# First loads on other queues, fewer and shorter dummy matmuls, and two transposes turned behind a product

## The chip, the cores and the metric

The kernel runs on one core of one Trainium2 chip. A core has a matrix engine (TensorE, in the profile PE for its matmuls and PEld for its weight loads), three engines for elementwise work (VectorE, DVE in the profile; ScalarE, ACT; GpSimd, POOL), and SyncE (SP), which here only issues transfers. ScalarE can issue transfers too. Each engine works through its own instructions in order and waits on semaphores for the others. The transfers of all queues are carried out by 16 DMA engines. The metric is the device time in microseconds (us); lower is better.

## What is computed

Attention with a polynomial sketch for 16 heads (4 batches of 4 heads, 1088 positions, 32 wide), and behind it a feed-forward layer with a squared ReLU:

```python
def phi(x):                                   # 64 features of each position
    a = einsum('rd,bhsd->bhsr', S1, x)        # S1, S2: 8 x 32
    b = einsum('rd,bhsd->bhsr', S2, x)
    return einsum('bhsi,bhsj->bhsij', a, b).reshape(..., 64)
q_p, k_p = phi(q), phi(k)
kv  = einsum('bhsf,bhsd->bhfd', k_p, v)
z   = sum(k_p, axis=2)
num = einsum('bhsf,bhfd->bhsd', q_p, kv)
den = einsum('bhsf,bhf->bhs', q_p, z)[..., None] + 1e-06
x   = (num / den).transpose(0, 2, 1, 3).reshape(4352, 128)
out = relu(x @ w_in) ** 2 @ w_out             # w_in 128 x 2048, w_out 2048 x 128
```

All arrays are float32.

## The kernel before, in words

The feed-forward part is by far the larger one: 4352 rows, cut into ten chunks (`FC`) of 256 to 512 columns of the transposed x, each going through 16 slices of 128 hidden units (lines 600 and 644). The attention of a batch has to be ready before the feed-forward of its rows. For most of the program an order of the instructions is planned by a small list scheduler (`_Order`), which is given durations and due times. The head of the program, which makes the first 256 columns of x from batch 0, is written out by hand, and the change lies in this head alone. Each engine runs the head's instructions in the order in which the source issues them.

What the head does, with the names that matter here:

- Loads. Before the change ScalarE's queue issues S1 and S2 into `s_nat` (L225, L226), 8 rows each. SyncE's queue issues, in this order: k of batch 0, columns 0 to 512 (the first range) and 512 to 1088 (the second range), each over 128 partitions (L181); the first part of q, 256 columns (L187); eight loads of v (L199), four for its first range of tiles (0 to 4) and four for its second (4 to 9); then more of q, the two weight matrices in quarters (L208, L217), the rest of q, and the loads of the next batches. Every transfer has one of eight semaphores, given out in turn in the order of the program. A transfer that gets a semaphore for the second time is issued only after the first transfer with it has landed; for SyncE the fourth load of v is the first of these.
- Dummies. TensorE has nothing to do until S has landed. `keep_warm(n, cols)` issues n matmuls of 128 x `cols` on constants, whose result nobody reads (L695). Seven of 512 columns stand ahead of the first real matmuls, and one of 384 behind them.
- S. Eight matmul instructions (L706) bring S1 and S2 into `sp`, in the forms in which they are used, and ScalarE copies that to `ss` (L709). Everything below needs `ss`.
- k. VectorE transposes k into `kt0` (L293, `a_kT0`): tiles 0 and 1, 2 and 3 (both of the first range), 4 to 6, 7 and 8 (of the second range). TensorE forms the sketch of k from it, in four groups `kf` of the same tiles (L318, `a_kf`), ScalarE copies one half of each (`kb`, L324), and VectorE multiplies the halves into `kp` (L334, `a_kp0`).
- q. VectorE transposes the first 256 columns of q (L299, `a_qT`), and TensorE forms both sketches of q with the 64 features spread out (L757, `q0`).
- kv and z. 72 matmul instructions sum kp times v over the nine tiles into `kvp` (L399, `a_kv0`), eight for each tile; those of tiles 0 to 3 need v's first range, the rest its second.
- Behind it follow, each short and each waiting for the one before: masks of kvp, den (L826), num (L831), the reciprocal, and the first 256 columns of `xT` (L854). Then the first feed-forward matmuls start (L600).

In the order of the source, VectorE transposes all of k, then q, and then forms the products `kp`. The lines that the listing does not explain by itself:

```python
W0, W1, W3 = 7, 0, 1                 # dummies: ahead of S, behind S, ahead of the first L600
new_kp(0)
a_kf(0, 2, psf, "po")                # TensorE, then ScalarE
a_qT(0, 0, 8)                        # VectorE
a_kp0(0, 2)                          # VectorE
```

Of the kernel before, what the change touches and what calls it, by code (L numbers as in the profile page):

```python
# [14 lines left out]
def _ap(t: bass.AP, p0: int, np_: int, off: int, free):  # L15
    p = list(t.ap)[0]
    return bass.AP(
        t.tensor, t.offset + p0 * p[0] + off, [[p[0], np_]] + [list(d) for d in free]
    )
# [88 lines left out]
def kernel(  # L108
# [11 lines left out]
    nc = tc.nc  # L120
# [7 lines left out]
    GT, G2, LA = 4, 6, 3.5  # L128
    LU = 4
    KC = [(0, 160), (160, 128)]  # L130
    W0, W1, W3 = 7, 0, 1
    ND, QT, WI, KL, QL = 2, 6.0, (1.0, 1.9), (30.0, 8.0), 4.0


# [25 lines left out]
    def sb(name, cols, dt=F32, rows=128):  # L160
        return cpool.tile([rows, cols], dt, tag=name, name=name)
# [10 lines left out]
    s_nat, ss, s2f = sb("s_nat", 32, rows=16), sb("ss", 80), sb("s2f", 32)  # L172
# [7 lines left out]
    def load_k(eng, b, c0=0, c1=S):  # L180
        eng.dma_start(  # L181
            kn[b % 2][:, c0:c1],
            bass.AP(k.tensor, k.offset + b * H * S * D + c0, [[G * D, 128], [1, c1 - c0]]),
        )

    def load_q(eng, b, c0, c1):
        eng.dma_start(  # L187
            qn[b % 2][:, c0:c1],
            bass.AP(q.tensor, q.offset + b * H * S * D + c0, [[G * D, 128], [1, c1 - c0]]),
        )  # L190
# [3 lines left out]
    def first(b, t, p):  # L194
        return NT * p + t if b else 4 * p + t if t < 4 else 16 + 5 * p + t - 4
# [26 lines left out]
            ),  # L222
        )

    nc.scalar.dma_start(s_nat[0:8, :], S1[:, :])  # L225
    nc.scalar.dma_start(s_nat[8:16, :], S2[:, :])  # L226
    load_k(nc.sync, 0, 0, 512)
    load_k(nc.sync, 0, 512, S)
    load_q(nc.sync, 0, 0, 256)
    for t0, t1 in ((0, 4), (4, NT)):  # L230
        for p in range(4):
            load_v(nc.sync, 0, p, t0, t1)
# [57 lines left out]
    def a_kT0(t0, n):  # L290
        p = 3 if t0 + n > NT - 2 else 4
        i = 32 * (first(0, t0, 1) - first(0, t0, 0))
        nc.vector.transpose(  # L293
            _ap(kt0, 0, 128, 128 * t0, [[32, p], [128, n], [1, 32]]),
            _ap(kn[0], 0, 128, 32 * first(0, t0, 0), [[i, p], [32, n], [1, 32]]),
        )

    def a_qT(b, i0, n):
        nc.vector.transpose(qT[:, 32 * i0 : 32 * i0 + 32 * n], qn[b % 2][:, 32 * i0 : 32 * i0 + 32 * n])  # L299
# [13 lines left out]
    def a_kf(t0, n, pool, tag, w=32):  # L313
        kf = pool.tile([128, 512], F32, tag=tag, name="kf")
        for t in range(n):
            for c in range(0, 128, w):
                o = 128 * (t0 + t) + c
                nc.tensor.matmul(  # L318
                    _ap(kf, c, w, 32 * t, [[32 * n, 2], [1, 32]]),
                    kt0[:, o : o + w],  # L320
                    sf,
                )
        kb = wpool.tile([128, 32 * 3], F32, tag="kb", bufs=4, name="kb")
        nc.scalar.copy(kb[:, 0 : 32 * n], kf[:, 32 * n : 64 * n])  # L324
        st["kf", t0] = kf, kb

    def new_kp(b):

        st[b, "kp"] = wpool.tile([128, 64 * NT * H], F32, tag="kp", name="kp")

    def a_kp0(t0, n):

        kf, kb = st["kf", t0]
        nc.vector.tensor_tensor(  # L334
            out=_ap(st[0, "kp"], 0, 128, 256 * t0, [[64, 4 * n], [8, 8], [1, 8]]),
            in0=_ap(kf, 0, 128, 0, [[8, 4 * n], [1, 8], [0, 8]]),
            in1=_ap(kb, 0, 128, 0, [[8, 4 * n], [0, 8], [1, 8]]),
            op=mult,
        )
# [352 lines left out]
    def keep_warm(n, cols=512):  # L692
        t_ = st["warm"]
        for _ in range(n):
            nc.tensor.matmul(  # L695
                t_[:, 0:cols],
                nc.const_aps.tensor(1.0, (128, 128), mybir.dt.bfloat16),
                nc.const_aps.tensor(1.0, (128, cols), mybir.dt.bfloat16),
            )
# [17 lines left out]
    for c in range(2, 4):  # L717
        load_wo(nc.sync, c)
    load_q(nc.sync, 0, 640, S)
    keep_warm(W1)  # L720
    keep_warm(1, 384)
    a_kT0(0, 2)
    a_kT0(2, 2)
    for x in range(2):
# [21 lines left out]
    nc.gpsimd.memset(_ap(pd, 0, 128, 8, [[9, 4 * NT], [1, 1]]), 1e-6)  # L746

    a_kT0(4, 3)
    a_kT0(7, 2)


    x0 = att("x0")
# [9 lines left out]
    qp0 = wpool.tile([128, 512], F32, tag="qp0", bufs=1, name="qp0")  # L762
    new_kp(0)
    a_kf(0, 2, psf, "po")
    a_qT(0, 0, 8)
    a_kp0(0, 2)
    a_kf(2, 2, psf, "pg")
    a_kf(4, 3, psf, "po")
    a_kf(7, 2, psf, "pg", 64)
# [402 lines left out]
```

## Time and profile before

| what | value |
|---|---|
| median of 3 runs | 183.94 us (183.80 to 184.47) |
| the profiled execution's own time | 184.05 us |
| its span, first to last instruction | 182.2 us |
| TensorE busy | 177.6 us, 97% of the span |
| VectorE, ScalarE, GpSimd busy | 121.8, 136.5, 38.6 us |
| first real matmul (L706) | at 4.08 us |
| sketch of k (L318), sketch of q (L757), kv (L399) start | at 4.94, 6.71, 7.33 us |
| first feed-forward matmul (L600) | at 12.32 us |

Times inside the profile count from the start of the span. The profiled execution's own time is 1.85 us longer than its span. A busy TensorE is not TensorE at its full speed, since its clock can be held at half; the profile gives the clock that was granted only as far as it was recorded. A wait of an instruction for several semaphores is put down to the one that came last by the profile, which need not be the real one.

### The profile page before, as it was taken

What the parts mean: (1) busy time and instruction counts of PE and PEld (TensorE: products, weight loads), DVE (VectorE), ACT (ScalarE), POOL (GpSimd) and SP (SyncE); (2) the same over time, 40 slices, a digit from 0 to 9 for tenths busy, and PEclk for the clock granted to TensorE, in tenths of its full rate; (3) what the DMA queues carried; (4) which work ended last, traced back from release to release, by engine and by line L of the source; (5) the groups of instructions that cost most, each with busy time, mean ns of one, the idle gap of its engine ahead of it and who ended that gap; (6) DMA issues with size and microseconds to landing.
All of it is one profiled execution on the core that took longest, in us unless ns stands there. A gap on an engine that the chain in (4) does not pass through costs nothing.

```text
span 182.2 us, 3996 instructions
## 1 busy us (share of the span) xinstructions
PE 177.6 (97%) x1529; PEld 104.7 (57%) x1529; DVE 121.8 (67%) x262; ACT 136.5 (75%) x259; POOL 38.6 (21%) x158
## 2 busy tenths in 40 slices
PE   7999999999999999999999999999999999999992
PEld 2868776656555655655555554545454555555792
DVE  4989779999999961899994335996353334333640
ACT  3439579759947886799937778995777777777980
POOL 3546118348200003470018000600000000000000
PEclk9999999999999999999999999999999999999999
DMA  5799995010028900000031200003003000300211
GB/s 167 199 275 324 213 261 136 8 31 0 0 43 217 204 0 4 4 2 0 0 54 23 35 0 5 0 0 59 0 4 58 0 0 6 51 0 0 35 26 29
DMA packets 26146, 11.26 MB, mean 62 GB/s; under 512 B 17936, under 2 KB 25104, under 8 KB 26128
## 3 DMA queue, kind: packets, MB, share of 16 engines
q1 hardware_dynamic: 25936, 10.95, 25.5%
q8 instruction: 12, 0.20, 0.5%
q10 hardware_dynamic: 192, 0.07, 0.1%
q14 instruction: 6, 0.05, 0.1%
HBM read 8.78 MB, written 2.23 MB: 60 GB/s over the span
## 4 chain that ended last, share of the span: by engine, by line
PE 96%; DMA 2%; DVE 0%; issue 0%; ACT 0%; ACTq 0%
PE po L644 61%; PE pg L600 18%; PE nd L553 3%; PE po L639 2%; PE pol L639 2%; PE qc L306 2%; DMA kn<-in_k_dram 2%; PE nd L417 1%; PE kvp L399 1%; PE kf L318 1%; PE qc L350 1%; PE kvp L417 1%; PE nd L350 0%; PE x L757 0%; PE den L826 0%; PE x L443 0%
## 5 line engine op out<-in xcount | busy, mean ns | idle before, releaser
L644 PE MATMUL po<-g,w_o 128*128 128x512 f32 (+3 forms) x288 | 122.7, 546 | 0.0
L612 ACT ACTIVATE gt<-pg 128x512 f32<-128x512 f32 (+3 forms) x144 | 75.2, 570 | 31.4 <-PE pg L600 30.9
L644 PEld LDWEIGHTS po<-g,w_o 128*128 128x128 f32 x288 | 53.4, 189 | 31.8 <-issue 24.8
L600 PE MATMUL pg<-xT,w_in 128*128 128x512 f32 (+3 forms) x160 | 70.0, 518 | 0.0
L623 ACT ACTIVATE g<-gt 128x512 f32<-128x512 f32 (+2 forms) x102 | 60.7, 623 | 1.6
L625 DVE TENSOR_TENSOR g<-gt 128x512 f32<-128x512 f32 (+3 forms) x43 | 30.0, 699 | 39.5 <-ACT gt L612 38.8
L600 PEld LDWEIGHTS pg<-xT,w_in 128*128 128x128 f32 x160 | 29.1, 190 | 28.8 <-ACT gt L612 11.6
L513 POOL COPY rd<-rc 32x9 f32<-32x9 f32 (+2 forms) x80 | 19.1, 239 | 26.8 <-DVE rc L505 23.5
L459 POOL COPY kv<-kvt 32x64 f32<-32x64 f32 x48 | 12.7, 264 | 44.7 <-DVE kvt L436 42.5
L522 DVE STREAM_SHUFFLE qa<-qc 128x576 f32<-128x576 f32 (+2 forms) x20 | 11.8, 648 | 0.0
L537 DVE TENSOR_TENSOR qp<-qa,qb 128x576 f32<-128x576 f32 (+2 forms) x20 | 10.8, 603 | 0.0
L485 DVE STREAM_TRANSPOSE qt<-qc 128x576 f32<-128x576 f32 (+2 forms) x10 | 5.8, 610 | 5.6 <-PE qc L350 3.8
L370 DVE TENSOR_TENSOR kp<-fs 128x576 f32<-128x576 f32 x12 | 8.7, 738 | 0.0
L648 DVE STREAM_TRANSPOSE oT<-po 128x512 f32<-128x512 f32 (+3 forms) x9 | 5.9, 653 | 2.1 <-PE po L644 2.1
L553 PE MATMUL nd<-qp,kv 32*32 32x288 f32 (+2 forms) x320 | 6.6, 354 | 0.0
L299 DVE STREAM_TRANSPOSE qT<-qn 128x192 f32<-128x192 f32 (+3 forms) x11 | 5.8, 555 | 0.6 <-DMA qn<-in_q_dram 0.6
L522 DVE STREAM_SHUFFLE qb<-qc 128x576 f32<-128x576 f32 (+2 forms) x10 | 6.1, 648 | 0.0
L570 DVE TENSOR_TENSOR xT<-nd,bc 128x576 fp32r<-128x576 f32 (+2 forms) x10 | 5.6, 592 | 0.5 <-PE nd L553 0.5
L639 PE MATMUL po<-w_o,g 128*128 128x128 f32 x32 | 5.8, 280 | 0.0
L639 PE MATMUL pol<-w_o,g 128*128 128x128 f32 x32 | 5.7, 275 | 0.0
L563 DVE STREAM_TRANSPOSE bc<-rd 128x576 f32<-128x576 f32 (+2 forms) x10 | 5.7, 596 | 0.0
L553 PEld LDWEIGHTS nd<-qp,kv 32*32 32x32 f32 x320 | 2.9, 103 | 3.6 <-issue 2.4
(106 smaller groups left out, 89.7 us busy)
## 6 DMA issues: line engine op xcount, KB each, us to landing
kn<-in_k_dram SPq DMA_DIRECT2D x3, 544.0 KB, 8.4
qn<-in_q_dram SPq DMA_DIRECT2D x3, 544.0 KB, 11.5
vn<-in_v_dram SPq DMA_DIRECT2D x9, 144.0 KB, 7.2
w_in<-in_moe_w_in_dram SPq DMA_DIRECT2D x4, 256.0 KB, 4.4
w_o<-in_moe_w_out_dram SPq DMA_DIRECT2D x4, 256.0 KB, 4.9
out_dram<-oT SPq DMA_DIRECT2D x12, 64.0 KB, 1.9
out_dram<-oT SPq DMA_DIRECT2D x8, 56.0 KB, 2.7
out_dram<-oT SPq DMA_DIRECT2D x8, 48.0 KB, 1.8
```

Source lines behind the costliest of these rows:

```text
L370: nc.vector.tensor_tensor(out=_ap(st[b, "kp"], 0, 128, 64 * NT * h, [[64, NT], [8, 8], [1, 8]]), in0=_ap(fs, 0, 128, o, [[32, NT], [1, 8], ...
L459: nc.gpsimd.tensor_copy(_ap(st[b, "kv"], 32 * c, 32, 64 * h, [[32, E], [1, 32]]), _ap(st["kvt"], 32 * h, 32, 0, [[64, E], [1, 32]]),)
L513: nc.gpsimd.tensor_copy(st[b, "rd", i0][32 * h : 32 * h + 32, n * c : n * c + n], st["rc"][32 * c : 32 * c + 32, n * h : n * h + n],)
L522: nc.vector.stream_shuffle(in_=banks(st[b, "qc", i0], 2 * x, 0, m), out=_ap(st[b, which, i0], 0, 128, 2 * m * x, [[m, 2], [1, m]]), mask=m ...
L537: nc.vector.tensor_tensor(out=st[b, "qp", i0, e][:, r], in0=st[b, f"qa{e}", i0][:, r], in1=st[b, "qb", i0][:, r], op=mult,)
L553: nc.tensor.matmul(nd[32 * h : 32 * h + 32, 512 * c : 512 * c + m], kv[r, o : o + 32], qp[r, m * h : m * h + m], start=(e == 0), stop=(e = ...
L600: nc.tensor.matmul(st["pg", u][:, n * i : n * i + n], w_in[:, 128 * (d0 + i) : 128 * (d0 + i) + 128], xT[:, c0 : c0 + n],)
L612: nc.scalar.activation(gt[:, 0:w], st["pg", u][:, 0:w], Relu)
L623: nc.scalar.activation(to, of, Square)
L625: nc.vector.tensor_tensor(out=to, in0=of, in1=of, op=mult)
L639: nc.tensor.matmul(po[x // 128][:, 0:128], g[:, x : x + 128], w, start=(d == 0), stop=(d == NB - 1),)
L644: nc.tensor.matmul(po[0][:, 0:n], w, g, start=(d == 0), stop=(d == NB - 1))
```

## The change

- k's first range and q's first part are issued by ScalarE's queue, in this order. S1 and S2 are issued by SyncE's queue, ahead of k's second range.
- Six dummies of 512 columns instead of seven stand ahead of the matmuls of S, and two of 160 columns instead of one of 384 behind them.
- On VectorE the transpose of k's last two tiles and the transpose of q stand behind the first product `kp`, no longer ahead of it.

The order of the semaphores follows the order of the program: k's first range now has the first, and the fourth load of v, which reuses it, waits for k's first range instead of S1. No other instruction is added, removed or moved on any engine; the planned part has the same order as before.

```diff
-    W0, W1, W3 = 7, 0, 1
+    W0, W1, W3 = 6, 1, 1
...
-    nc.scalar.dma_start(s_nat[0:8, :], S1[:, :])
-    nc.scalar.dma_start(s_nat[8:16, :], S2[:, :])
-    load_k(nc.sync, 0, 0, 512)
+    load_k(nc.scalar, 0, 0, 512)
+    nc.sync.dma_start(s_nat[0:8, :], S1[:, :])
+    nc.sync.dma_start(s_nat[8:16, :], S2[:, :])
     load_k(nc.sync, 0, 512, S)
-    load_q(nc.sync, 0, 0, 256)
+    load_q(nc.scalar, 0, 0, 256)
...
-    keep_warm(W1)
-    keep_warm(1, 384)
+    keep_warm(W1 + 1, 160)
     a_kT0(0, 2)
     a_kT0(2, 2)
...
     a_kT0(4, 3)
-    a_kT0(7, 2)
...
     new_kp(0)
     a_kf(0, 2, psf, "po")
+    a_kp0(0, 2)
+    a_kT0(7, 2)
     a_qT(0, 0, 8)
-    a_kp0(0, 2)
     a_kf(2, 2, psf, "pg")
```

## The prediction, made before the changed kernel was run

> **What bounds the kernel now.** The page comes first: how much of the span is TensorE (PE), and which chain ended last.
>
> ```profile
> PE 177.6 (97%) x1529; PEld 104.7 (57%) x1529; DVE 121.8 (67%) x262; ACT 136.5 (75%) x259; POOL 38.6 (21%) x158
> PE 96%; DMA 2%; DVE 0%; issue 0%; ACT 0%; ACTq 0%
> ```
>
> PE is busy for 177.6 of 182.2 us. None of the edits touches what runs after 13 us, so they can only move the moment from which PE has feed-forward work without a break (the first L600 at 12.32), and the end moves with it one for one. Next, the chain of waits in order of time, asked for the first 25 us (start, duration, what):
>
> ```profile
> 0.73 2.82 DMA kn<-in_k_dram
> ...
> 4.08 0.49 PE sp L706 x8
> 4.57 0.43 PE warm L695
> 5.01 1.77 PE kf L318 x64
> 6.78 0.62 PE x L757 x16
> 7.40 2.25 PE kvp L399 x72
> ```
>
> From 4.08 on the chain is PE without a gap up to the end of kvp (9.65); from there a string of short steps leads to 12.3, and the change doesn't touch it. So the question is when kvp ends. The timeline of the head says what each engine does (start, duration, engine, what; in brackets the idle time before and who ended it):
>
> ```profile
> 0.73 0.89 SPq L181 DMA_DIRECT2D kn<-in_k_dram  x2
> 0.73 0.60 ACTq L225 DMA_DIRECT2D s_nat<-in_S_dram  x1
> 0.77 3.15 PE L695 MATMUL warm<-const-bfloat16-1.0 128*128 128x512 bf16 x7 [0.77 <-PEq L1156]
> 1.37 0.29 ACTq L226 DMA_DIRECT2D s_nat<-in_S_dram  x1
> 3.58 0.77 DVE L293 STREAM_TRANSPOSE kt<-kn 128x256 f32<-128x256 f32 x2 [1.00 <-DMA kn<-in_k_dram]
> 4.08 0.49 PE L706 MATMUL sp<-sel,s_nat 16*32 16x80 f32 x8 [0.17 <-DVE kt L293]
> 4.54 0.84 DVE L293 STREAM_TRANSPOSE kt<-kn 128x384 f32<-128x384 f32 x2 [0.19 <-DMA kn<-in_k_dram]
> 4.63 0.23 ACT L709 COPY ss<-sp 128x80 f32<-128x80 f32 x1 [1.45 <-PE sp L706]
> 5.30 0.40 DVE L299 STREAM_TRANSPOSE qT<-qn 128x256 f32<-128x256 f32 x1
> 5.90 2.75 DVE L334 TENSOR_TENSOR kp<-kf,kb 128x512 f32<-128x512 f32 x4 [0.20 <-ACT kb L324]
> 6.71 0.69 PE L757 MATMUL x<-qT,sq 32*64 32x256 f32 x16
> ```
>
> Last, single lines and their waits; the rows of PEldq are TensorE's queue holding for semaphores, and the last two belong to the eighth load of v:
>
> ```profile
> L706 PEldq EVENT_SEMAPHORE  x2: 51/51/51, 2.2 to 4.0; - x2
> ...
> L318 PE MATMUL kf<-ss,kt x64: 219/314/316, 4.9 to 6.6; 128*32 128x64 f32 x56, 128*64 128x64 f32 x8
> ...
> L399 PEldq EVENT_SEMAPHORE  x4: 51/51/51, 6.7 to 8.1; - x4
> ...
> L199 SPq DMA_DIRECT2D vn<-in_v_dram x1: 430/430/430, 5.5 to 5.5; - x1
> ...
> DMA to landing us min/median/max: 2.6/2.6/2.6
> ```
>
> Three readings. (1) sp waited for S2: its queue holds until 2.2 (S1) and until 4.0 (S2), so the 0.17 that the timeline puts down to DVE is S2's landing. The dummies cover this: they start 0.43 apart, and the seventh ends at 3.7. (2) The matmuls of kf fall from 314 to 219 ns within the group; in the trace their bundles stand 0.107 apart up to 5.98 and 0.056 after it. PE runs at half speed until 5.98 (the page's clock row reads full throughout and doesn't show it). (3) kvp's second half (40 of 72 matmuls) waits for v's second range. Its last load was issued at 5.46 and landed 2.6 later, at 8.1; that half started at 7.33 + 32 x 0.029 = 8.25. From a release to the first load sp needed 0.08 (3.97 to 4.05), so the half could have started at 8.20: only 0.05 of slack.
>
> **The change, part by part.** I carry the sum on the profiled execution: 184.05 us, of them 182.2 span and 1.85 around it. It stands 0.11 above the median of the three runs (183.94).
>
> S1 and S2 first on SyncE, six dummies. S1, first on its queue, was seen by PE 1.5 after its issue; S2, issued 0.64 later behind the traffic of k, 2.6 after. An issue of 128 rows takes SP 0.43; S2's eight rows took ACT 0.29. On SP, S2 is issued at about 0.73 + 0.40 = 1.1, before most of k's traffic. Bounds for its arrival: 2.6 (S1's latency) and 3.7 (its own latency again). I take 3.2, the middle, since k's first range is issued at the same moment as before. Six dummies end at 0.77 + 6 x 0.43 = 3.35, so sp starts there and not at 4.08: -0.73. Two dummies of 160 columns (0.27 at half speed) replace one of 384 (0.32), between sp and the copy to ss, where PE waits anyway: nothing; without that wait they would cost 0.27. ss follows at 3.90 and kf could start at 4.20 (before 4.93).
> The Trainium skill, "DMA: Bandwidth & Descriptors", section "Issuing engines are not separate DMA queues", speaks against this step: transfers from all issuing engines share the same 16 DMA engines, so another queue saves issuing time only. By that rule alone S2 gains its 0.3 of earlier issue, kf would start at about 4.6, and the sum carried through DVE would be 184.3 instead of 184.2; the trace neither proves nor refutes it, since S1 (alone) and S2 (in traffic) differ by 1.1 in latency. The outcome with S2 late is rival A.
>
> k's first range first on ScalarE. SP's first issue took 0.41, ACT's first 0.60 (L225). So k lands between 3.55 (as now) and 3.74; I take 3.74, because L225 is the same place in the same queue. kt's first transpose ends 0.45 later and kf starts at 4.25: -0.68. ACT's table load (1.28) and the 0.20 copy slide from 1.69 to about 1.85 and end at 3.35, ahead of ss at 3.90: nothing; an issue 0.5 longer would use up that cover. q's first part landed at 5.04 and is now read at about 6.1: nothing.
>
> k's second range third on SP. Issue about 1.5 instead of 1.2, behind k's first range in the DMA engines as before. Landing between 4.51 (unmoved) and 5.04 (q, which took the 0.53 behind it, goes first). I take 4.70, k's own shift, because the first range holds the engines until then either way.
>
> kf, the order on DVE. kf's first two groups run at half speed from 4.25 to 5.1; kb is ready 0.94 after kf's start (5.87 before), at 5.19. DVE from k's landing: transpose of three tiles 0.50 (5.20), first kp 0.61 (5.81), last transpose 0.26 (6.07), qT 0.40 (6.47), three kp 2.14: 8.61, before 8.65. The swap fills the 0.20 that DVE idled ahead of the first kp, and that is all it gives. Behind the moved kp wait kf's last group (needs the transpose of 6.07) and L757 (needs qT): L757 at 6.57 and not 6.71, kvp at 7.19 and not 7.33: -0.14.
>
> v behind a new wait. On SP the fourth load of v reuses the semaphore of the first transfer in program order: S1 before, k's first range now. It was issued at 3.56; now it waits for k's landing, 3.74 to 3.76: +0.20. The other loads of v, the rest of q and all weights are queued behind it on SP; the weights have room (first cast 10.86, needed by 12.26). Bounds: 0 (k lands at 3.55) to +0.20. If the eighth load moves by 0.19 with it, it lands at 8.29 and kvp's second half starts at 8.39: +0.14 on 8.25. Its last kp (8.61) is in time for 9.09.
>
> Sum: PE and DVE would be 0.14 earlier, v makes it 0.14 later, and the later one decides: 184.05 + 0.14 = 184.19 in a profiled execution, 184.1 against the median. What the earlier S wins (0.73) is lost at two other landings: k's second range through DVE, and v's second range.
>
> **Rivals.**
> A, S2 lands no earlier. For: reading (1). Against: it is issued ahead of most of k. Then kf starts at 4.93 and the first kp at 5.90, but the last transpose and qT (0.66) now follow it: DVE ends 9.30, L757 starts at 7.2, kvp 0.5 late: 184.4.
> B, slower: TensorE stays at half speed. The clock rose at 5.98, after a stretch from 2.57 with 3.24 of 3.41 us counted busy (windows of the profile). The change removes 0.43 of dummies and opens gaps ahead of kf (0.25), at k's second range (0.2) and at the last transpose. If these are too many, PE stays slow for another such stretch, to 9.39: kf's rest +0.5, L757 +0.45, kvp twice as slow until then; kvp ends at about 10.95, not 9.65: 183.94 + 1.3 = 185.2. It decides where PE idles more than the window allows; before, 5 to 10% was allowed, now I count 14 to 20%. For the 3.41 stretch: the Trainium skill, "TensorE: Matmul & The Clock Gate" (Part 1), says the throttle is released after a busy, free-running window of about 3.4 us; the trace has one rise, at 5.98, which fits a window that began at 2.57.
> C, v is not late. SP spends 0.29 on each S instead of 0.43, k lands at 3.55, and the fourth load of v is not held. Then the -0.14 of PE stands, or -0.3 with a k that is early too: 183.7.
> D, clearly faster: the whole 0.73 arrives at the end and the half-speed stretch costs less behind it. This needs both ranges of k and v to land 0.7 earlier, while v's loads are issued 0.47 apart as before: 183.94 - 0.95 = 183.0.
>
> **How the numbers follow.** Chances: forecast 0.42, A 0.15, B 0.15, C 0.20, D 0.08. Half a per cent (0.92 us) is about what a measurement of this kernel can tell from no change. Forecast and C lie within it; so does A, except 0.02 in which its delay and some slow clock add up. Faster 0.08 (D), slower 0.17 (B and that share), same 0.75. The range takes the forecast, A, C and most of B: 183.3 to 185.2; D and the tail of B stay out. The likeliest case's own range is 183.8 to 184.4, from v's bounds (0 to +0.20) and the spread of the runs.
>
> **What would show it.** Right: TensorE's queue released for sp before 3.4; sp at 3.35 and kf near 4.25; the second k landing within 4.5 to 5.0 and no idle DVE ahead of the first kp; fourth load of v issued right after k's landing, L399's second half released at 8.2 to 8.4; kvp ending within 0.2 of 9.65. Wrong: S2 released near 4.0 (A); matmuls of L399 at half their speed (B); the eighth load of v well before 8.1 with kvp following it (C, D).

## The result, and the profile after

The changed kernel takes 186.06 us (median of 22 runs, 184.33 to 187.32); the kernel before, run beside it, 184.75 (22 runs, 183.80 to 185.83). The ratio is 1.0059, with a 95% interval of 1.0036 to 1.0083: slower, by an estimate just over the half per cent that the prediction set as its limit, with an interval that reaches to both sides of it; the median lies outside the prediction's range. The ratios in this document are of fast runs alone, without those more than 1.5% above the fastest of the same kernel (here one, of 187.32), which is why this one is below the ratio of the medians, 1.0071. The spread of the runs is part of the result: 3.0 us after, 2.0 before.

The profiled execution of the changed kernel happened to be one of its faster ones: 184.58 us, span 182.7, against 184.05 and 182.2 before. Its page comes first, with the engines and the chain that ended last:

```profile
PE 177.3 (97%) x1529; PEld 104.7 (57%) x1529; DVE 121.9 (67%) x262; ACT 136.6 (75%) x259; POOL 39.2 (21%) x158
PE 91%; DMA 5%; SPq 1%; POOL 0%; issue 0%; DVE 0%
```

PE's work is the same, but 5% of the chain is now transfers instead of 2%. The timeline of the head says which (start, duration, engine, what; idle time before it and who ended it):

```profile
0.73 0.41 SPq L226 DMA_DIRECT2D s_nat<-in_S_dram  x1
0.74 0.39 ACTq L181 DMA_DIRECT2D kn<-in_k_dram  x1
...
1.20 0.29 SPq L227 DMA_DIRECT2D s_nat<-in_S_dram  x1
...
1.53 0.36 SPq L181 DMA_DIRECT2D kn<-in_k_dram  x1
...
3.67 0.49 PE L706 MATMUL sp<-sel,s_nat 16*32 16x80 f32 x8 [0.18 <-DMA s_nat<-in_S_dram]
...
4.50 1.64 PE L318 MATMUL kf<-ss,kt 128*32 128x64 f32 x56
...
4.88 0.58 DVE L293 STREAM_TRANSPOSE kt<-kn 128x384 f32<-128x384 f32 x1 [0.64 <-DMA kn<-in_k_dram]
...
6.59 0.45 PE L318 MATMUL kf<-ss,kt 128*64 128x64 f32 x8 [0.45 <-DVE kt L293]
...
6.97 0.69 PE L755 MATMUL x<-qT,sq 32*64 32x256 f32 x16
...
7.59 2.32 PE L399 MATMUL kvp<-vn,kp 128*64 128x64 f32 x72
...
12.04 2.09 POOL L688 CAST w_in<-w_in 128x512 fp32r<-128x512 f32 x3 [4.52 <-DMA w_in<-in_moe_w_in_dram]
```

The matmuls of S start at 3.67 (before 4.08) and those of kf at 4.50 (4.94), so 0.4 is won at the front. Then VectorE idles 0.64 for k's second range, which lands at 4.84 (before 4.51); PE idles 0.45 ahead of kf's last group; and the sketch of q (line 755 here, 757 before) starts at 6.97, 0.26 later than before. From there kvp runs as before. In this execution the first quarter of w_in lands only at 11.98 (10.81 before), and the first feed-forward matmul waits about 0.45 more for its cast; it starts at 13.03 (12.32 before).

That the median lies 1.5 above this execution is not explained by it. So seven more executions of the changed kernel were profiled (after_again, after_p1 to after_p6). The trace records the granted clock of TensorE from the moment at which it first rises to full speed; that moment is the column "rise".

| execution | clock rise | k's 2nd range landed | kvp (L399), first and last start | first L600 | own time | own time - first L600 |
|---|---|---|---|---|---|---|
| before | 5.98 | 4.51 | 7.32, 9.42 | 12.32 | 184.05 | 171.73 |
| after_p3 | 4.14 | 4.76 | 7.41, 9.51 | 12.41 | 183.99 | 171.58 |
| after | 5.38 | 4.84 | 7.58, 9.68 | 13.03 | 184.58 | 171.55 |
| after_again | 9.48 | 4.84 | 8.38, 10.96 | 13.85 | 185.47 | 171.62 |
| after_p5 | 9.70 | 5.11 | 8.42, 11.08 | 13.98 | 185.63 | 171.65 |
| after_p2 | 9.84 | 5.68 | 9.00, 11.46 | 14.36 | 186.12 | 171.76 |
| after_p1 | 10.19 | 4.74 | 8.31, 11.24 | 14.14 | 186.03 | 171.89 |
| after_p4 | 11.82 | 5.37 | 8.69, 12.19 | 15.09 | 186.71 | 171.62 |
| after_p6 | 12.25 | 4.79 | 8.48, 12.27 | 15.17 | 186.80 | 171.63 |

(The times in the table are cut, not rounded, to hundredths, so they can be 0.01 below those in the lines of the profile.) The last column is constant within 0.35: what sets these executions apart happens ahead of the first L600. And of the eight executions of the same program the two whose clock rose by 5.4 lie at 184.0 and 184.6, the six whose clock rose after 9.4 at 185.5 to 186.8. The landing of k's second range doesn't sort them like that: it came earliest in after_p1 (4.74) and at 4.79 in after_p6, which took 186.03 and 186.80. One line of the kernel shows where the time goes. L399's matmuls in after_p3 (duration of one in ns, minimum, median and maximum; first and last start):

```profile
L399 PE MATMUL kvp<-vn,kp x72: 222/222/270, 7.4 to 9.5; 128*64 128x64 f32 x72
```

and in after_p4:

```profile
L399 PE MATMUL kvp<-vn,kp x72: 221/314/369, 8.7 to 12.2; 128*64 128x64 f32 x72
```

In after_p4 the 72 matmuls need 3.5 us from first to last start instead of 2.1, and they also start 1.28 later, 0.6 of it because k's second range landed later in this execution (5.37 against 4.76), as its timeline shows:

```profile
4.55 1.08 PE L318 MATMUL kf<-ss,kt 128*32 128x64 f32 x32
...
5.41 0.58 DVE L293 STREAM_TRANSPOSE kt<-kn 128x384 f32<-128x384 f32 x1 [1.08 <-DMA kn<-in_k_dram]
...
6.13 1.55 PE L318 MATMUL kf<-ss,kt 128*32 128x64 f32 x32 [0.49 <-DVE kt L293]
...
7.61 1.16 PE L755 MATMUL x<-qT,sq 32*64 32x256 f32 x16
...
8.70 3.72 PE L399 MATMUL kvp<-vn,kp 128*64 128x64 f32 x72
```

L755 takes 1.16 at half speed, 0.69 at full speed. The prediction's rival B is this case; it got a chance of 0.15 and a price of 1.3.

### The profile page after: what moved, and what is told of

It is laid out like the page before. It is cut to its first block, busy times and chain, and to the rows that moved or that the text cites. A ratio compares the mean times of both kernels' runs of the same rounds, so it can differ in the third digit from the quotient of the medians.

```text
span 182.7 us, 3996 instructions
## 1 busy us (share of the span) xinstructions
PE 177.3 (97%) x1529; PEld 104.7 (57%) x1529; DVE 121.9 (67%) x262; ACT 136.6 (75%) x259; POOL 39.2 (21%) x158
## 4 chain that ended last, share of the span: by engine, by line
PE 91%; DMA 5%; SPq 1%; POOL 0%; issue 0%; DVE 0%
PE po L644 61%; PE pg L600 18%; PE nd L553 3%; DMA w_in<-in_moe_w_in_dram 3%; PE po L639 2%; PE pol L639 2%; PE qc L306 2%; DMA kn<-in_k_dram 1%; PE nd L417 1%; SPq L199 1%; PE qc L350 1%; PE kvp L417 1%; PE nd L350 0%; POOL w_in L688 0%; PE warm L844 0%
## 5 line engine op out<-in xcount | busy, mean ns | idle before, releaser
L600 PE MATMUL pg<-xT,w_in 128*128 128x512 f32 (+3 forms) x160 | 70.1, 519 | 0.0
L600 PEld LDWEIGHTS pg<-xT,w_in 128*128 128x128 f32 x160 | 29.2, 190 | 28.4 <-ACT gt L612 11.5
L513 POOL COPY rd<-rc 32x9 f32<-32x9 f32 (+2 forms) x80 | 19.7, 246 | 25.8 <-DVE rc L505 22.6
L522 DVE STREAM_SHUFFLE qa<-qc 128x576 f32<-128x576 f32 (+2 forms) x20 | 11.8, 649 | 0.0
```

Source lines behind the costliest of these rows:

```text
L513: nc.gpsimd.tensor_copy(st[b, "rd", i0][32 * h : 32 * h + 32, n * c : n * c + n], st["rc"][32 * c : 32 * c + 32, n * h : n * h + n],)
L522: nc.vector.stream_shuffle(in_=banks(st[b, "qc", i0], 2 * x, 0, m), out=_ap(st[b, which, i0], 0, 128, 2 * m * x, [[m, 2], [1, m]]), mask=m ...
L600: nc.tensor.matmul(st["pg", u][:, n * i : n * i + n], w_in[:, 128 * (d0 + i) : 128 * (d0 + i) + 128], xT[:, c0 : c0 + n],)
```

## The experiments

Two theories stood at the start. *Clock:* the missing seventh dummy and the new gaps let TensorE's clock rise late in a part of the executions. *Landings:* the new queues make k's second range (or w_in) land later, whatever the clock does. Ratios are to the kernel before, run beside each kernel on the same chip, with 95% intervals; each kernel was run 9 to 12 times unless said otherwise.

**Each of the three edits alone.**

e_loads, the queues alone:

```diff
-    nc.scalar.dma_start(s_nat[0:8, :], S1[:, :])
-    nc.scalar.dma_start(s_nat[8:16, :], S2[:, :])
-    load_k(nc.sync, 0, 0, 512)
+    load_k(nc.scalar, 0, 0, 512)
+    nc.sync.dma_start(s_nat[0:8, :], S1[:, :])
+    nc.sync.dma_start(s_nat[8:16, :], S2[:, :])
...
-    load_q(nc.sync, 0, 0, 256)
+    load_q(nc.scalar, 0, 0, 256)
```

> The change of the queues alone (k's first range and q's first part on ScalarE's queue, S1 and S2 on SyncE's), dummies and order as before. Measured so far: the whole change has a ratio of 1.0059 to the kernel before, and its executions spread over 3.0 us (184.3 to 187.3) where those of before spread over 2.0 (183.8 to 185.8). Clock theory (the change leaves TensorE at half speed longer in part of the executions, by fewer dummies and more gaps): with seven dummies nothing is lost, ratio 0.998 to 1.002, spread 2. Loads theory (k's second range and the first quarter of w_in land later, because q's first part goes beside them on another queue): ratio 1.003 to 1.006, k's second range landing at 4.8 to 4.9 instead of 4.5, L757 from 6.9.

Measured: 1.0017 [0.9985, 1.0050], median 184.64. In its profile the clock rises at 4.47 and k's second range lands at 5.78; the timeline shows what that does:

```profile
4.69 0.65 PE L318 MATMUL kf<-ss,kt 128*32 128x64 f32 x32
...
5.81 0.84 DVE L293 STREAM_TRANSPOSE kt<-kn 128x384 f32<-128x384 f32 x2 [1.50 <-DMA kn<-in_k_dram]
...
6.53 0.93 PE L318 MATMUL kf<-ss,kt 128*32 128x64 f32 x32 [1.19 <-DVE kt L293]
```

VectorE idles 1.50 and PE 1.19 for that landing. In this execution it is the landing alone, with a clock that was full in time. Over the twelve runs the cost of the queues is not clear of nothing; the ratio lies where the clock theory had put it.

e_dummies, the dummies alone:

```diff
-    W0, W1, W3 = 7, 0, 1
+    W0, W1, W3 = 6, 1, 1
...
-    keep_warm(W1)
-    keep_warm(1, 384)
+    keep_warm(W1 + 1, 160)
```

> The dummies alone: six of 512 columns ahead of S instead of seven, two of 160 behind instead of one of 384; queues and order as before. S lands at 4.0 as before, so TensorE idles from 3.35 to 4.05. Clock theory: ratio 1.004 to 1.010, executions spread over 3 us, in part of them the matmuls of kvp run at half speed. Loads theory: ratio 0.998 to 1.002, nothing but the dummies differs in the trace.

Measured: 1.0029 [1.0001, 1.0057], median 185.07. The profiled execution (185.61) has its clock rise at 10.14, although its loads are those of before and k's second range lands at 4.28. Its timeline:

```profile
3.89 0.49 PE L706 MATMUL sp<-sel,s_nat 16*32 16x80 f32 x8 [0.40 <-DMA s_nat<-in_S_dram]
...
8.08 3.24 PE L399 MATMUL kvp<-vn,kp 128*64 128x64 f32 x72
```

PE idles 0.40 for S2 where the seventh dummy used to stand, and kvp runs mostly at half speed. In this execution it is the clock alone. The ratio is below what the clock theory expected (1.004 to 1.010), and its interval just clears 1.

e_order, the order on VectorE alone:

```diff
-    a_kT0(7, 2)
...
-    a_qT(0, 0, 8)
     a_kp0(0, 2)
+    a_kT0(7, 2)
+    a_qT(0, 0, 8)
```

> The order on VectorE alone: first product kp ahead of the transpose of k's last tiles and of q; queues and dummies as before. Both theories: S decides the first product (5.90), so the two transposes (0.66) slide behind it, L757 starts at 7.2 instead of 6.7 and kvp ends 0.5 later: ratio 1.002 to 1.004. Clock theory adds that TensorE's longer gap ahead of kf's last group can cost more in some executions; loads theory adds nothing.

Measured: 1.0018 [0.9985, 1.0050], median 184.60. The clock rises at 5.70, the loads are those of before (second range at 4.17), and still kvp starts 0.57 later than before in the two profiles. Its timeline:

```profile
6.38 0.37 DVE L293 STREAM_TRANSPOSE kt<-kn 128x192 f32<-128x192 f32 x1
...
6.89 0.45 PE L318 MATMUL kf<-ss,kt 128*64 128x64 f32 x8 [0.70 <-DVE kt L293]
...
7.28 0.69 PE L756 MATMUL x<-qT,sq 32*64 32x256 f32 x16
```

With k's last transpose behind the first kp, PE idles 0.70 ahead of kf's last group; before it had none there. The three single ratios add up to 1.0064, near the 1.0059 of the whole, though each interval alone reaches to 1 or nearly so.

**Two edits, and the dummies back.** e_loads_order, queues and order together with the old dummies (the diffs of e_loads and e_order):

> The change with the dummies of before (seven of 512, one of 384): queues and order changed. Clock theory: what remains is the later landing of k's second range (0.26 at kvp), ratio 1.000 to 1.003, spread 2. Loads theory: as the whole change, ratio 1.004 to 1.007.

Measured: 1.0050 [1.0015, 1.0085], median 185.45. The rise is at 4.15, the second range lands at 5.35, the first L600 starts at 12.95. So seven dummies don't undo the change, as the loads theory had expected. This run can't say which of the two edits costs it: kvp starts at 7.96, only 0.07 later than with the new order alone (e_order, 7.89), and 0.24 earlier than with the new queues alone (e_loads, 8.20).

**More dummies.** e_fill, the change with seven dummies in front and small ones of 128 columns in the gaps of kf:

```diff
-    W0, W1, W3 = 6, 1, 1
+    W0, W1, W3 = 7, 1, 1
...
     a_kf(2, 2, psf, "pg")
+    fill(2)
     a_kf(4, 3, psf, "po")
+    fill(5)
     a_kf(7, 2, psf, "pg", 64)
+    fill(1)
```

> The changed kernel with TensorE kept busy: seven dummies of 512 columns instead of six, and eight dummies of 128 columns in the waits of the sketch of k and ahead of that of q (two, five and one; 0.107 each at half speed, in waits of 0.25, 0.6 and 0.1). Queues and order as in the change. What the traces showed so far: the clock rose at the end of stretches of 3.41 us in which matmuls streamed for 0.80 to 0.95 of the time, and didn't rise after stretches of 0.74 and 0.69. Clock theory: the executions with a mean clock of 0.991 (7 of 22) and those above 186.7 (5 of 22) go; median 184.4 to 185.0, spread 2. Loads theory: the later landing of k's second range remains and the dummies only add work: median as the change (186.0) or above.

Measured: 1.0062 [1.0028, 1.0097], median 185.72, lowest 185.00 (after: 184.33). The rise is at 5.99. From its timeline:

```profile
5.94 0.58 DVE L293 STREAM_TRANSPOSE kt<-kn 128x384 f32<-128x384 f32 x1 [1.58 <-DMA kn<-in_k_dram]
...
7.14 0.46 PE L754 MATMUL x<-const-bfloat16-1.0 128*128 128x128 bf16 x5
...
8.07 0.69 PE L763 MATMUL x<-qT,sq 32*64 32x256 f32 x16
```

The median meets neither theory (184.4 to 185.0, or 186.0 and above). The rise is early and the profiled execution still takes 185.91, because the second range landed at 5.91, because the fills now stand on PE's path (from the end of k's last transpose to the sketch of q it takes 0.70, against 0.52 in after_p3), and because 172.2 instead of 171.6 follow behind the first L600. Work put in to hold the clock has to fit into the gap as it is in each execution, and this one didn't.

e_four, the kernel before with four dummies (`W0 = 4`) and nothing else:

> The kernel before with four dummies of 512 columns ahead of S instead of seven, all else as before: TensorE idles from 2.5 to 4.05, and nothing that the data path waits for is touched. Clock theory: a stretch of 3.41 us can pass only from about 3 us on, so the clock rises at 6.5 to 10 instead of 4 to 7.2: median 1.0 to 1.8 above before (ratio 1.005 to 1.010). Loads theory: no difference, ratio 0.998 to 1.002.

Measured: 1.0034 [1.0003, 1.0065], median 185.37 in 10 runs, lowest 184.84. The rise is at 9.70, kvp takes 2.8 us from first to last start, the first L600 is at 13.83. Taking dummies from the kernel before, without touching a load or VectorE, gives the late clock again, where the clock theory had put it (6.5 to 10); the ratio is below the 1.005 that it had expected at least.

**Which load matters.** e_q_sync, the change with q's first part left on SyncE:

> The change with q's first part left on SyncE's queue, behind k's second range, as before; all else as in the change. Loads theory: k's second range lands at 4.2 to 4.6 again (with q on ScalarE's queue 4.8, 5.8 and 5.4), the first kp moves up by 0.2 to 0.4, and the median falls to 184.6 to 185.2. Clock theory: fewer gaps on TensorE, so a part of the loss goes, but six dummies remain: median 185.2 to 185.8, some executions with a clock of 0.991 or above 186.7 remain.

Measured: 1.0027 [0.9998, 1.0057], median 185.10; rise at 8.22, second range at 4.80. The loads theory had the median right, but not by its own way: it had expected the landing back at 4.2 to 4.6. e_q_sync_fill, the same with the dummies of e_fill:

> Both: q's first part on SyncE's queue, seven dummies, and the eight dummies in TensorE's waits. Both theories: no later than either alone, median 184.0 to 184.6, ratio 0.996 to 1.000. Where clock and loads each cost something, it is the fastest of the four; if one theory is wrong, it equals the run without that part.

Measured: 1.0057 [1.0031, 1.0084], median 185.40; rise at 5.26, second range at 5.04. Both theories had put it at 0.996 to 1.000, and both missed: an early clock and q on SyncE together don't bring the time back. e_q_only, the kernel before with q's first part issued by ScalarE behind S1 and S2:

```diff
-    load_q(nc.sync, 0, 0, 256)
+    load_q(nc.scalar, 0, 0, 256)
```

> The kernel before with one edit: q's first part on ScalarE's queue, behind S1 and S2, instead of SyncE's behind k's second range. Dummies, order, S and k as before. Loads theory: two queues are served in turn, so q takes the DMA engines' time from k's second range, which lands at 4.7 to 5.6 (with all of k and q on one queue: 4.2 to 4.5 in four traces), DVE's chain follows, ratio 1.002 to 1.005. Clock theory alone: seven dummies, clock rises by 7.2 at the latest, ratio 0.998 to 1.002.

Measured: 0.9989 [0.9957, 1.0021], median 184.14; rise at 6.00, second range at 4.26. There q is issued at 1.71, after k's second range (1.20), and costs nothing. The loads theory had expected a landing at 4.7 to 5.6 from q on another queue alone, and that form of it is refuted. e_swap, the queues of the change, but q left on SyncE (old dummies, old order):

> The kernel before with k's first range on ScalarE's queue and S1, S2 on SyncE's, nothing else: q stays on SyncE's queue behind k's second range, seven dummies, old order. Loads theory: k's second range lands at 4.5 to 5.0 (issued 0.33 later), S at 3.5 instead of 3.9; DVE is bound by k, so ratio 0.999 to 1.003. Clock theory: clock rise at 3.5 to 6.9, as before; ratio 0.998 to 1.001.

Measured: 1.0002 [0.9977, 1.0028], median 184.36; rise at 5.01, second range at 4.92. The sketch of q starts at 6.53, the earliest of all, and what comes next is the very wait that the prediction named as its likeliest end, from the timeline:

```profile
7.34 1.15 PE L399 MATMUL kvp<-vn,kp 128*64 128x64 f32 x32
...
8.68 1.39 PE L399 MATMUL kvp<-vn,kp 128*64 128x64 f32 x40 [0.18 <-DMA vn<-in_v_dram]
```

kvp's second half waits for v. It is real, but binds only where everything ahead of it is early. e_q_sync_seven, e_swap with the new order on VectorE:

> The same with the order of the change (first kp ahead of the last transpose and q): the change without the move of q's first part and without the new dummies, that is, without both suspected costs. Both theories together: ratio 0.998 to 1.002, no execution with a clock of 0.991. Loads theory alone (dummies don't matter): as the change with q on SyncE's queue, 1.002 to 1.005. Clock theory alone (q doesn't matter): as the queues and order changed with seven dummies, 1.003 to 1.007, or 1.000 if that loss was chance.

Measured: 1.0018 [0.9983, 1.0052], median 184.88; rise at 4.16, second range at 5.05. This is the kernel of e_q_sync_fill without the fills and with the old dummies, so the extra dummies there seem to cost more than they save, though the intervals overlap. One of its twelve runs has a mean clock of 0.991, where none was expected.

**The changed kernel again, for its spread.** after_again is the changed kernel, run twelve times more; after_p1 to after_p6 are single profiled executions of it.

> The changed kernel once more, on the same chip as the three others: ratio 1.004 to 1.008 by both theories; clock theory: a part of the executions at 0.991 or above 186.7; loads theory: k's second range landing at 4.8 to 5.9 in its trace.

Measured: 1.0067 [1.0030, 1.0105], median 186.59, 184.14 to 187.49. The profiled execution has its rise at 9.48.

> The changed kernel, one profiled execution. If its mean clock is 0.991 and the clock theory holds, the record shows a rise before 5, a fall one or two stretches later, and a second rise 3.41 us after that, with kvp at half speed (3.0 instead of 2.1 us) and a time of 185.5 to 187. With a clock of 0.997 to 1.000: a rise before 6.1 and 184.1 to 185.5, or a rise at 8 to 10 and 185.5 to 187.5.

> The same, another execution: a mean clock of 0.991 goes with a rise, a fall and a second rise; a rise at 8 to 10 with 185.5 to 187.5; a rise before 6.1 with 184.1 to 185.5.

> The same, another execution: a mean clock of 0.991 goes with a rise, a fall and a second rise; a rise at 8 to 10 with 185.5 to 187.5; a rise before 6.1 with 184.1 to 185.5.

> The same, another execution: a mean clock of 0.991 goes with a rise, a fall and a second rise; a rise at 8 to 10 with 185.5 to 187.5; a rise before 6.1 with 184.1 to 185.5.

Measured: 186.03, 186.12, 183.99 and 186.71, with rises at 10.19, 9.84, 4.14 and 11.82; the kernel before took 184.09 beside them.

> The changed kernel once more, one profiled execution. Six profiled executions of it so far: clock rise at 4.14, 5.38, 9.48, 9.84, 10.19 and 11.82 us, time 183.99, 184.58, 185.47, 186.03 to 186.12 and 186.71. If the time is set by the rise alone, this one lies on the same line: a rise by 6.0 gives 184.0 to 184.6, a rise after 9.4 gives 185.4 to 186.8. Open is where the executions with a mean clock of 0.991 (13 of 34) spend their 3.4 us at half speed: if one of them is met here, the theory says that they rise before 6.0 and fall back for one 3.41 us stretch in the first 20 us; the rival says that the fall lies later, in the FFN.

> As the run before it: rise by 6.0, 184.0 to 184.6; rise after 9.4, 185.4 to 186.8; a mean clock of 0.991, an early rise and one stretch back at half speed.

Measured: 185.63 with a rise at 9.70, and 186.80 with a rise at 12.25; both on the line drawn by the others. The kernel before, beside them, took 186.41 once.

What follows from all of them. With seven dummies in front, nine kernels were profiled once each, and all nine clocks rose by 6.0. With six or four, eleven executions were profiled, and nine rose at 8.2 or later. So the number of dummies moves the rise. A second part is the order on VectorE, which alone starts kvp 0.57 later in its trace (e_order). The third is the landing of k's second range. In the five profiles in which SyncE's queue issues k's first range ahead of it, as before (before, e_dummies, e_order, e_four, e_q_only), it landed at 4.17 to 4.51. With k's first range on ScalarE and q on SyncE (four profiles) it landed at 4.80 to 5.05; with both on ScalarE (eleven) at 4.74 to 5.91. Its issue alone moved by 0.33, from 1.20 to 1.53. The parts can't be added up cleanly: the dummies alone cost 0.29%, queues and order alone 0.50%, the whole 0.59 and 0.67%, with intervals of 0.2 to 0.4% either way. Clock and landing probably meet, since the wait for k's second range is a gap on PE too: the twelve runs of e_loads_order fall into six of 184.27 to 185.10 and six of 185.80 to 187.34 (two of these with a mean clock of 0.991). Its only trace is of the first kind, so that is argued and not shown.

What stays open. In 13 of the 34 runs of the changed kernel in two sets of repeated runs (22 and 12) the recorded mean clock was 0.988 to 0.991, which is about one stretch of 3.4 us at half speed (0.009 x 183 x 2 = 3.3); they took 185.4 to 187.2. None of the eight profiled executions is such a one, so where they lose it isn't known. The kernel before has such runs too, but fewer: 8 of the 102 that ran beside the experiments, at 185.9 to 188.4; each other kernel has none to two in 9 to 12. They are not the main loss: without them the medians are 185.5 for the changed kernel (21 runs) and 184.4 for the one before (94). Nor is it known why the first cast of w_in starts, right after its landing, at 11.9 to 12.0 in after, e_loads and e_q_sync and at 9.6 to 11.5 elsewhere; it is the reason for some 0.45 in the profile of after. And the last column of the table, constant there, is 172.0 to 172.4 in the profiles of e_fill, e_q_sync_fill, e_q_only and e_q_sync_seven: up to 0.8 can also be lost behind the head, and these runs don't say where.

## Why the prediction was wrong, by its own steps

- *S1 and S2 first on SyncE, S2 at 3.2, sp at 3.35 (-0.73): mis-sized.* S2 landed at 3.53 to 3.72 in the eight executions, the upper end of the bounds (2.6 to 3.7), and sp started at 3.67 to 3.86: 0.2 to 0.4 won. The middle between S1's latency (alone) and S2's (in traffic) was the wrong choice: S2 is issued at 1.20 with k's first range already under way (issued at 0.74), and its 2.3 to 2.5 from issue to landing lie near the loaded 2.6 of before. The Trainium skill, "DMA: Bandwidth & Descriptors", section "Issuing engines are not separate DMA queues", holds that another queue saves issuing time only, and by that rule the prediction had put kf at about 4.6; it started at 4.49 to 4.68, so that figure was the better forecast. The trace doesn't agree with the rule to the letter: S2 was issued 0.17 earlier than before (1.20 against 1.37) and landed 0.2 to 0.4 earlier (before 3.95).
- *k's first range, landing at 3.74: wrong by a price.* ScalarE's first issue took 0.39, not the 0.60 of L225 before, and k landed at 3.43 to 3.60. kt was ready and S2 set kf's start.
- *k's second range at 4.70, bounds 4.51 to 5.04: right as a mechanism, too narrow in size.* It landed at 4.74 to 5.68, in three of eight above 5.04. The upper end was put at q's landing of before, and that wasn't an upper bound: q's first part, now on the other queue, landed at 3.83 to 4.50, ahead of k's second range in every one of the eight.
- *L757 at 6.57 and not 6.71: wrong in sign.* Even in the best execution (after_p3, a full clock from 4.14 on) it started at 6.80. The chain of waits of that execution (start, duration, what):

```profile
1.53 3.24 DMA kn<-in_k_dram
...
4.79 0.58 DVE kt L293
5.37 0.62 DVE kp L334
5.99 0.29 DVE kt L293
6.29 0.14 issue
6.42 0.45 PE kf L318 x8
6.87 0.62 PE x L755 x16
7.49 2.25 PE kvp L399 x72
```

  The moved kp stands in the middle of this chain, ahead of k's last transpose, and kf's last group and the sketch of q follow that transpose in a row. The prediction let L757 wait for qT instead of the last group, but with the group it would have come to the same: 6.07 + 0.14 + 0.38 = 6.59. Of the 0.23 by which it was out here, 0.09 is the landing (the transpose starts at 4.79, not 4.70). Another 0.11 is the last transpose: the prediction took 0.26 for it, the distance to the next start on VectorE, but kf's matmuls wait for its end, 0.37 after its start (5.91 to 6.28). So 0.38 won at kf's start has become 0.09 lost at the start of L755.
- *The fourth load of v behind a new wait, +0.20, kvp's second half at 8.39: didn't decide.* Since k landed at 3.5, the load was issued at 3.45 to 3.61 (before 3.56), and the eighth landed at 7.48 to 8.19, not 8.29. kvp itself was later.
- *The sum, 184.19 in a profiled execution:* with an early rise the two executions gave 183.99 and 184.58, on both sides of it, the second outside the 183.8 to 184.4 of the likeliest case. That the sum lies between them is luck as far as its terms go: -0.14 on PE came out as +0.09 and +0.26, and v's +0.14 didn't decide. And an early rise isn't the typical run.
- *Rival B, 0.15 and 185.2: this is the step that failed most.* The mechanism was named rightly, with its place and its sign. Three things were missed. First, it was treated as yes or no for the kernel, from a stretch that starts at 2.57. That start belongs to one execution only: the position of the stretches differs from one execution to the next, so the question was in how many executions the kernel passes, not whether it does. Second, its price: a rise at 9.39 was counted at 1.3 us. Executions with a rise at 9.5 to 10.2 took 1.4 to 2.1 us more than the profile of before, and those with a rise at 11.8 and 12.3 took 2.7 more, because nearly the whole of kvp then runs at half speed; in after_p2 and after_p4 a late landing of k (5.68, 5.37) is part of it. Third, its measure can't tell: it counted idle time by the profile's busy windows, and by these a stretch with 3.13 of 3.41 us busy ended in a rise (after_p3), while one with 3.21 (e_q_sync) and one with 3.17 (after_p4) didn't. How much of the loss over all runs is this step and how much the -0.14 of PE and VectorE, which was a loss too, stays open, since the kernel with the old dummies (e_loads_order) still has 1.0050.
- *D, everything 0.73 earlier:* not seen in any run. The lowest of 40 runs of the changed kernel, after_p3 among them, is 183.99; the lowest of before is 183.69.

Why did the kernel fail so often? A rough reckoning from the traces: count a matmul as streaming from its start for as long as its columns take at the clock of the moment (the 512-column dummies start 0.43 apart at half speed; 64 float32 columns of kf 0.107, twice as much a column). In the stretch of 3.41 us that ended with the rise, PE streamed for 0.82 of the time in before, 0.80 in after and 0.82 in after_p3. The stretches that were passed by without a rise had 0.78 and 0.69 in after_p4, 0.75 and 0.73 in after_p6, 0.73 in after_again, 0.69 in e_dummies, 0.62 in e_four. Over all 20 executions no stretch up to 0.75 ended in a rise, every one of 0.80 and more did, and between them both are seen (e_q_sync rose after 0.78 and had failed at 0.79), so the limit can't be read sharply, but lies near 0.8. The seven dummies keep nearly every position of the stretch above that: the reckoning gives 0.82 or more for the kernel before at all starts from 0.4 to 2.7 us. For the changed kernel, by its traces with a late rise, it is 0.79 to 0.84 only for starts near 0.7 to 0.9, 0.74 to 0.80 from 1.2 to 2.1, and less behind: six dummies have streamed by 3.3, S2 comes at 3.6, and every gap behind it counts. That is worked out from traces and not a measurement of the limit itself; what is measured is the rise and the time for each number of dummies.

## What to carry to other kernels

A warm-up should be sized to the latest moment at which the real work can start, and for every position of the clock's stretch, not for the one profile at hand: one dummy of 0.43 us less, which nobody waited for, and two small ones behind brought, by themselves, a rise 4 us later and 1.6 us in the one execution of each kernel that was profiled, and 0.3% over all runs. Ahead of a change to a kernel's head, profile the same kernel several times: where its runs spread by 2 us, as here, one profile shows one of several cases. And a load that is moved to another queue to bring one transfer forward can push another back, as here k's second range; look at what lands second. Last, a step on an engine's chain that another engine waits for counts to its end, not to the next start.

## What the runs showed of the hardware

- *The clock's stretches run free of the kernel.* In all 20 profiled executions the recorded full speed lasted either 177.49 or 174.08 us, which is 52 or 51 times 3.413, and for one and the same program the rise lies anywhere from 4.14 to 12.25 us after the start of the span. The Trainium skill, "TensorE: Matmul & The Clock Gate", Part 1, says that the window is 3413 ns, free-running and doesn't reset when a kernel starts, which agrees; it puts the variation of the transition at 500 ns either way, and here it was 8 us, by the reckoning above because a stretch that is a little too empty costs a whole further one.
- *A late rise doesn't show on the page.* The clock row reads full throughout, and the mean clock of after_p4 is 1.000, since the record starts with the rise. The median duration of one matmul (222 against 314 ns for L399) shows it.
- *The first issue of a queue has no fixed price.* ScalarE's first issue took 0.60 when it was S1 (before) and 0.39 when it was k's first range (after), in the same place.
